# W2 staged in seven buffers, batch 1's third row block after group 0's last add, and earlier sums in the last group

## The chip, the cores and the metric

The kernel runs on one core of a Trainium2 chip. The metric is the device time of one execution in microseconds (us). The kernel before has a median of 313.59 us over six runs (312.78 to 314.56).

The engines are named as in the profile: PE is TensorE's matmuls and PEld its weight loads, DVE is VectorE, ACT is ScalarE, POOL is GpSimd, SP is SyncE, which here only issues transfers. DMA engines move data between HBM and the on-chip memory SBUF; matmuls write to PSUM.

## The reference

Two stages, eight batches of 576 positions, eight heads of 64, model width 512, hidden width 2048:

```python
def _attn_ref(q, k, v):                       # [8, 8, 576, 64] each
    scores = (1.0 / np.sqrt(D)) * np.matmul(q, k.transpose(0, 1, 3, 2))
    rel = pos[:, None] - pos[None, :]
    mask = (rel >= 0) & (rel < 64)            # a causal window of 64 positions
    scores = np.where(mask, scores, -1e9)
    attn = softmax(scores)
    return np.matmul(attn, v)

def _moe_ref(x, g_ln, w_ch1, w_ch2):          # x: [8, 576, 512], heads side by side
    xn = (x - mean) / np.sqrt(var + 1e-06) * g_ln
    ch = np.maximum(xn @ w_ch1, 0.0) @ w_ch2  # 512 -> 2048 -> 512
    return x + ch
```

Inputs and output are float32; the kernel computes its matmuls in float16 with float32 sums in PSUM.

## The kernel before, in words

**Tiling.** The first 512 positions of each batch make a group of four row blocks of 128 (`kb` or `j` 0 to 3): groups 0 to 7. The last 64 positions of all eight batches together make group 8, the last one. For a row block, `s_mm` makes the scores with 16 small matmuls (PE, L283) and their exponentials (ACT, L290), `s_mask` multiplies the mask in (DVE, L297), and `b_step` does 16 matmuls with V (PE, L317, into the one PSUM tile `xps`) and then, on DVE, the reciprocal of the sums (L320), the division into `xn` (L323), mean and variance (L325, L328) and, in groups 0 and 1, `z` (L338). From group 2 on `z_step` makes `z` on POOL (L342 to L345). `zt_step` brings `z` into `zT`, by PE and ACT (L357, L360) or by a transposing DMA (L353).

**The MLP of a group.** `mlp_units` gives a list of units, each some matmuls. Group 0: eight half blocks (`l1_half`, L528, eight matmuls each), eight whole blocks of the first layer (`l1`, L392), nine units `l2_two` (L543) that do the second layer of row blocks 0 and 1 together, piece by piece of W2, and eight units `l2` (L404) for row blocks 2 and 3, four parts each. After a row block's last part `add_out` adds the result to `xn` (DVE, L414), which frees the PSUM buffer, and `store` sends the rows out on SP's queue (L430). Group 1 has sixteen half blocks and sixteen `l2` parts. Groups 2 to 8 do the second layer in seven products instead of eight (`stage`, L469) with sums of the hidden activations `sS` (`s_sums`, DVE, L443) and sums of W2, `wT`, which `w2_sums` writes late in group 1 and in group 2. PSUM has two buffers `mm`, which hold the blocks `hps`, `hph`, `ch`, `pA` and `pB` in turn.

**Order.** There is no scheduler: each engine runs its instructions in the order in which the program was written out. At the end of the kernel a loop walks the units of group g; `at(i, f, ...)` puts work of the next batches (attention, loads, casts) behind unit i. Work put behind one unit runs in the order of the `at` calls.

**Loads and weights.** All loads go out on SP's queue, one after another, and a load waits there until its buffer is free. POOL casts everything to float16. W2 comes in eight pieces of 512 KB: `w2_load(i)` into one of the four buffers of the pool `pwst` (tag `wld`), `w2_cast(i)` into `w2s` (POOL, L201). Four loads were written first (L795), and load i + 4 after cast i (L800 to L803). Unit i of `l2_two` uses piece i for row block 0 and piece i - 1 for row block 1. The same four buffers hold `sS` from group 2 on. The tiles `wT[2]`, `wT[3]`, `wT[4]` are each as large as a piece, 4 KB in each partition.

**The last group.** Group 8 has its own order (`plan` in `mlp_units`): its first layer also runs in seven products (`l1_product`, L578), whose parts are kept by ACT (L590), added by DVE (L593) and rectified by DVE, POOL (L595) or ACT (L617). The second layer's stages follow, with `s_sums` between them: `s_sums(c0, c1, n)` makes sum n for chunks c0 to c1.

Of the kernel before, what the change touches and what calls it, by code (L numbers as in the profile page):

```python
# [10 lines left out]
FP32 = mybir.dt.float32  # L11
# [9 lines left out]
def kernel(  # L21
# [12 lines left out]
    DM = H * D  # L34
# [7 lines left out]
    XQ = 3  # L42
# [4 lines left out]
    p_wst = ctx.enter_context(tc.tile_pool(name="pwst", bufs=4))  # L47
# [23 lines left out]
    wT = {i: p_const.tile([128, NHC // 2, DM // 2], FP16, tag=f"wT{i}", name=f"wT{i}") for i in (2, 3, 4)}  # L71
# [119 lines left out]
                                    op0=ALU.mult, op1=ALU.mult)  # L191

    def w2_load(i):
        t = p_wst.tile([128, 2, DM], FP32, tag="wld", name=f"w2s_{i}")
        wst[("w2", i)] = t
        nc.sync.dma_start(
            out=t, in_=moe_w_ch2[256 * i:256 * (i + 1), :].rearrange("(c p) d -> p c d", p=128),
        )
# [184 lines left out]
    def mlp_units(g, split=0, two=False, seven=True):  # L383
# [48 lines left out]
        def s_sums(c0, c1, *which):  # L432
            if not sS:
                for n in range(1, 5):
                    sS[n] = p_wst.tile([128, NHC // 2, 256], FP16, tag="wld", name=f"sS{n}_{g}")
            c = slice(c0, c1)
            a11, a12 = hv[:, c, 0, 0:256], hv[:, c, 1, 0:256]
            a21, a22 = hv[:, c, 0, 256:512], hv[:, c, 1, 256:512]
            s1, s2, s3, s4 = (sS[n][:, c, :] for n in range(1, 5))
            for n in which:  # L440
                o, x, y, op = {1: (s1, a21, a22, ALU.add), 2: (s2, s1, a11, ALU.subtract),
                               3: (s3, a11, a21, ALU.subtract), 4: (s4, a12, s2, ALU.subtract)}[n]
                nc.vector.tensor_tensor(out=o, in0=x, in1=y, op=op)  # L443
# [40 lines left out]
        def stage(n, p):  # L484
            product(n, p)
            if last and n == 3:
                post_c(0, p)
                if p:
                    store_rest(0, slice(256, DM), None)
                return  # L490
            if p == 0:
                return
            if n == 1:
                post("A", 0, 0)
            elif n == 2:
                post("B", 0, 0)
                if last:
                    store_rest(0, slice(0, 256), nc.sync)
            elif n == 6:
                post("A", 0, 1)  # L500
            elif n == 7:
                post("A", 2, 1)
                if last:
                    post_c(2, 0)
                    post_c(2, 1)
                else:
                    post("C", 2, 1)
                post("A", 2, 0)
            elif n == 4:
                post("B", 2, 0)  # L510
                if last:
                    store_rest(2, slice(0, DM), None)
                else:
                    store(2)
                    store(3)
            elif n == 3:
                post("C", 0, 1)
                tbank["shared"] = False
                tbank["n"] = 0
                store(0)  # L520
                store(1)
# [89 lines left out]
        def l1_c(d):  # L611
            l1_product(7, d)
            l1_sum(l1_quad(d, 1, 1), "A", "s5", d)
# [5 lines left out]
        if last:  # L619
            def plan():  # L620
                yield
                l1_b(0)
                for d in range(1, 4):
                    l1_a(d)
                    l1_c(d - 1)
                    l1_b(d)
                    l1_e(d - 1)
                s_sums(0, 4)
                stage(1, 0)
                l1_c(3)  # L630
                s_sums(0, 4, 1)
                s_sums(4, 8, 1)
                stage(1, 1)
                l1_e(3)
                s_sums(0, 4, 2)
                stage(2, 0)
                s_sums(4, 8, 2)
                stage(2, 1)
                stage(6, 0)
                s_sums(0, 4, 3)  # L640
                stage(6, 1)
                s_sums(4, 8, 3)
                stage(5, 0)
                s_sums(0, 4, 4)
                stage(5, 1)
                s_sums(4, 8, 4)
                for n in (7, 4, 3):
                    for p in range(2):
                        stage(n, p)
                yield  # L650
            l1_a(0)
            return plan(), s_sums
# [139 lines left out]

    load_qk(1, 0)
    load_v(1, 0, 2)
    for i in range(4):  # L795
        w2_load(i)
    cast_qk(1, 0)
    cast_v(1, 0, 1)
    cast_v(1, 1, 2)
    for i in range(8):  # L800
        w2_cast(i)
        if i < 4:
            w2_load(i + 4)  # L803
    load_qk(1, 1)
    load_v(1, 2, 4)
    cast_qk(1, 1)
# [13 lines left out]
    for g in range(NGRP):  # L820
# [4 lines left out]
        units, s_sums = mlp_units(g, (8, 16)[g] if g < 2 else 0, g == 0, g > 1)  # L825
        slots = [[] for _ in range(len(units) + 1)]

        def at(i, f, *a):
            slots[min(i, len(slots) - 1)].append((f, a))

        b = g + 1
        if g == 0:
            at(0, b_step, 0, 3)
            at(1, zt_step, 0, 2)
            at(3, zt_step, 0, 3)
            at(4, newton, 0, 0, 4)
            at(11, t_main, 1, 0, 0, 1)
            at(12, t_main, 1, 1, 0, 1)
            at(13, vB_cur, 1, 0, 1)
            at(13, vB_prev, 1, 0, 1)  # L840
            at(13, vB_cur, 1, 1, 1)
            at(13, vB_prev, 1, 1, 1)
            at(16, s_mm, 1, 0)
            at(16, s_mask, 1, 0)
            at(17, s_mm, 1, 1)
            at(17, s_mask, 1, 1)
            at(18, b_step, 1, 0)
            at(21, b_step, 1, 1)
            at(22, zt_step, 1, 0)
            at(24, zt_step, 1, 1)  # L850
            at(26, t_main, 1, 0, 1, 0)
            at(27, t_main, 1, 1, 1, 1)
            at(28, vB_cur, 1, 2, 0)
            at(28, vB_prev, 1, 2, 1)
            at(29, vB_cur, 1, 3, 0)
            at(29, s_mm, 1, 2)
            at(29, s_mask, 1, 2)
            at(30, s_mm, 1, 3)
            at(30, s_mask, 1, 3)
            at(30, load_v, 2, 0, 4)  # L860
            at(31, b_step, 1, 2)
        if g == 1:
            at(0, cast_qk, 2, 0)
            at(0, cast_qk, 2, 1)
            at(1, b_step, 1, 3)
            at(2, zt_step, 1, 2)
            at(13, newton, 1, 0, 4)
            at(5, zt_step, 1, 3)
            at(4, alloc_v, 2)
            at(4, alloc_qkT, 2)  # L870
            at(4, alloc_vB, 2)
            at(5, cast_v, 2, 0, 4)
            at(5, make_vB, 2)
            at(4, t_main, 2, 0, 0)
            at(4, t_main, 2, 1, 0)
            at(6, t_main, 2, 0, 1)
            at(6, t_main, 2, 1, 1)
            at(25, w2_sums, 3, 0, 4)
            at(28, w2_sums, 3, 4, 8)
            for j in range(4):  # L880
                at((9, 13, 16, 19)[j], s_mm, 2, j)
                at((10, 14, 17, 20)[j], s_mask, 2, j)
                at((13, 17, 20, 23)[j], b_step, 2, j)
                at((13, 17, 20, 23)[j], z_step, 2, j)
                at((18, 21, 24, 27)[j], zt_step, 2, j)
            at(3, load_qk, 3, 0)
            at(4, load_qk, 3, 1)
            at(7, load_v, 3, 0, 4)
            at(8, alloc_qkT, 3)
            at(8, cast_qk, 3, 0)  # L890
            at(10, cast_qk, 3, 1)
            at(14, alloc_v, 3)
            at(14, cast_v, 3, 0, 2)
            at(14, cast_v, 3, 2, 4)
            at(17, alloc_vB, 3)
            at(17, make_vB, 3)
            at(31, s_mm, 3, 0)
            at(31, s_mask, 3, 0)
            for i, (x, half) in zip((12, 24, 12, 28), ((0, 0), (1, 0), (0, 1), (1, 1))):
                at(i, t_main, 3, x, half, 0)  # L900
            at(40, load_qk, 4, 0)
            at(40, load_qk, 4, 1)
            at(40, load_v, 4, 0, 4)
# [28 lines left out]
        if g > 1 and n < B:  # L932
            at(16, cast_qk, n, 1, (1,) if n >= XQ else (0, 1))
            at(20, alloc_v, n)
            at(20, cast_v, n, 0, 2)
            at(21, cast_v, n, 2, 4)
            at(21, alloc_vB, n)
            at(21, make_vB, n)
            for i, (x, half) in zip((13, 17, 13, 21) if n >= XQ else (17, 19, 21, 25),
                                    ((0, 0), (1, 0), (0, 1), (1, 1))):  # L940
                at(i, t_main, n, x, half, 0)
            at(27, s_mm, n, 0)
            at(28, s_mask, n, 0)
            if n + 1 < B:
                at(40, load_qk, n + 1, 0)
                at(40, load_qk, n + 1, 1)
                at(40, load_v, n + 1, 0, 4)
# [60 lines left out]
```

The softmax here doesn't subtract the row's maximum and nothing guards it: scores larger than these inputs give would overflow.

## Time and profile before

The profiled execution took 314.48 us, of which 312.7 us lie between its first and its last instruction (the span).

| engine | busy us | share of the span |
|---|---|---|
| PE | 298.3 | 95% |
| DVE | 217.9 | 70% |
| POOL | 170.8 | 55% |
| ACT | 153.1 | 49% |

Costly groups of instructions on PE: L392 96.3 us (416 matmuls, 380 ns each as recorded, overlapping), L404 23.1 us, L528 23.4 us. W2's loads take 5.1 us each from issue to landing, in the median of the eight. The granted clock of PE was 0.998 of full speed on the mean.

A timeline row gives start, duration, engine, line, operation, out<-in, shapes and count; a row of several instructions covers them from the first start to the last end. Brackets hold the idle time of the engine just before it and what ended it. Matmuls overlap, so each is recorded longer than the step to the next one.

### The profile page before, as it was taken

What the parts mean: (1) busy time and instruction counts of PE and PEld (TensorE: products, weight loads), DVE (VectorE), ACT (ScalarE), POOL (GpSimd) and SP (SyncE); (2) the same over time, 40 slices, a digit from 0 to 9 for tenths busy, and PEclk for the clock granted to TensorE, in tenths of its full rate; (3) what the DMA queues carried; (4) which work ended last, traced back from release to release, by engine and by line L of the source; (5) the groups of instructions that cost most, each with busy time, mean ns of one, the idle gap of its engine ahead of it and who ended that gap; (6) DMA issues with size and microseconds to landing.
All of it is one profiled execution on the core that took longest, in us unless ns stands there. A gap on an engine that the chain in (4) does not pass through costs nothing.

```text
span 312.7 us, 7625 instructions
## 1 busy us (share of the span) xinstructions
PE 298.3 (95%) x3089; PEld 198.4 (63%) x3089; DVE 217.9 (70%) x411; ACT 153.1 (49%) x258; POOL 170.8 (55%) x255
## 2 busy tenths in 40 slices
PE   7988989899999999999999989999999999999992
PEld 4556535598454468646954776459646855788882
DVE  0687675856665996589666945896569685877882
ACT  2486624487326742866157526772375048315500
POOL 7578666454951798279805964598236506204300
PEclk9999999999999999999999999999999999999999
DMA  8999999999776996897189997993690393003013
GB/s 192 270 386 288 336 310 283 290 293 217 148 170 201 248 185 127 264 293 123 34 258 286 194 151 203 322 144 64 203 183 17 53 205 132 2 0 136 0 37 101
DMA packets 109893, 57.43 MB, mean 184 GB/s; under 512 B 79841, under 2 KB 100833, under 8 KB 109858
## 3 DMA queue, kind: packets, MB, share of 16 engines
q1 hardware_dynamic: 108800, 53.75, 69.5%
q0 software_dynamic: 768, 2.80, 3.7%
q8 instruction: 24, 0.39, 0.5%
q10 hardware_dynamic: 290, 0.40, 0.4%
q14 instruction: 11, 0.09, 0.1%
HBM read 38.80 MB, written 9.44 MB: 154 GB/s over the span
## 4 chain that ended last, share of the span: by engine, by line
PE 69%; DMA 12%; DVE 7%; POOL 4%; SPq 4%; issue 2%; ACT 1%; POOLq 0%; ACTq 0%
PE hps L392 23%; PE pA L469 9%; PE pC L469 7%; PE pB L469 6%; PE ch L404 6%; DMA qk<-in_k_dram 4%; DMA w2s<-in_moe_w_ch_dram 4%; PE hph L528 4%; PE xps L317 3%; PE sc L283 3%; DVE sS L443 2%; PE lA L578 2%; SPq L141 2%; PE tp L226 2%; DMA zT<-z 2%
## 5 line engine op out<-in xcount | busy, mean ns | idle before, releaser
L392 PE MATMUL hps<-zT,w1g 128*128 128x512 f16 x416 | 96.3, 380 | 0.0
L396 ACT ACTIVATE hrT<-hps 128x512 f16<-128x512 f32 x104 | 62.3, 599 | 38.6 <-PE hps L392 35.1
L392 PEld LDWEIGHTS <-w1g 128*128 128x128 f16 x416 | 38.3, 98 | 41.9 <-issue 0.9
L290 ACT ACTIVATE pt<-sc 128x512 f16<-128x512 f32 x72 | 39.0, 595 | 28.9 <-DVE xn L476 15.6
L469 PEld LDWEIGHTS <-sS 128*128 128x128 f16 x448 | 43.1, 98 | 5.7 <-DVE sS L443 0.7
L342 POOL TENSOR_SCALAR rsz<-mvg 128x1 f32<-128x1 f32 x28 | 10.7, 382 | 60.0 <-DVE mvg L328 59.4
L128 POOL CAST qk<-qk 128x1024 f16<-128x1024 f32 x32 | 34.9, 1102 | 13.4 <-DMA qk<-in_k_dram 7.2
L469 PEld LDWEIGHTS <-hrT 128*128 128x128 f16 x336 | 32.5, 98 | 5.3 <-ACT hrT L617 0.3
L212 ACT COPY qkT<-tp 128x1024 f16<-128x1024 f16 x16 | 16.1, 1012 | 34.6 <-PE tp L226 25.5
L297 DVE TENSOR_TENSOR pt<-pt,mask 128x1024 f16<-128x1024 f16 x32 | 26.0, 818 | 9.2 <-ACT pt L290 9.1
L476 DVE TENSOR_TENSOR xn<-pA,xn 128x512 f32<-128x512 f32 x28 | 19.2, 686 | 18.4 <-PE pA L469 18.4
L345 POOL TENSOR_SCALAR z<-xn,rsz 128x512 f16<-128x512 f32 x28 | 25.0, 892 | 4.6 <-DMA zT<-z 1.8
L469 PE MATMUL pA<-wT,sS 128*128 128x256 f16 x224 | 27.1, 273 | 0.2 <-DVE sS L443 0.2
L469 PE MATMUL pC<-w2s,sS 128*128 128x256 f16 x224 | 26.8, 273 | 0.0
L320 DVE RECIPROCAL rcp<-xps 128x8 f32<-128x8 f32 x36 | 7.4, 205 | 26.7 <-PE xps L317 26.7
L325 DVE BATCH_NORM_STATS2 stats<-xn 128x6 f32<-128x512 f32 x36 | 25.0, 695 | 1.2
L323 DVE TENSOR_TENSOR xn<-xps,rcp 128x512 f32<-128x512 f32 x36 | 24.9, 691 | 1.2
L528 PE MATMUL hph<-zT,w1g 128*128 128x256 f16 x192 | 23.4, 273 | 2.1 <-ACT zT L360 1.1
L443 DVE TENSOR_TENSOR sS<-hrT 128x512 f16<-128x512 f16 (+1 forms) x40 | 24.5, 614 | 0.6 <-ACT hrT L396 0.6
L404 PE MATMUL ch<-w2s,hrT 128*128 128x512 f16 x96 | 23.1, 380 | 0.0
L528 PEld LDWEIGHTS <-w1g 128*128 128x128 f16 x192 | 18.2, 98 | 5.1 <-issue 2.2
L317 PEld LDWEIGHTS <-pt 128*64 128x64 f16 x576 | 12.2, 110 | 13.7 <-issue 5.7
(108 smaller groups left out, 450.5 us busy)
## 6 DMA issues: line engine op xcount, KB each, us to landing
out_dram<-xn SPq DMA_DIRECT2D x33, 256.0 KB, 2.8
qk<-in_q_dram SPq DMA_DIRECT2D x16, 512.0 KB, 6.4
qk<-in_k_dram SPq DMA_DIRECT2D x16, 512.0 KB, 7.4
v<-in_v_dram SPq DMA_DIRECT2D x32, 256.0 KB, 6.5
w2s<-in_moe_w_ch_dram SPq DMA_DIRECT2D x12, 512.0 KB, 5.7
w1s<-in_moe_w_ch_dram SPq DMA_DIRECT2D x4, 512.0 KB, 6.7
tk<-in_k_dram SPq DMA_DIRECT2D x8, 256.0 KB, 4.6
tv<-in_v_dram SPq DMA_DIRECT2D x8, 256.0 KB, 5.7
```

The source lines that it names most:

```text
L128: nc.gpsimd.tensor_copy(out=dst[:, :].rearrange("p (a j) e d -> p a e j d", j=j), in_=t[:, :].rearrange("p (a e j d) -> p a e j d", e=2, j ...
L290: nc.scalar.activation(out=o, in_=i, func=AF.Exp, bias=0.0, scale=scale)
L297: nc.vector.tensor_tensor(out=ptv, in0=ptv, in1=mb, op=ALU.mult)
L323: nc.vector.tensor_tensor(out=xn, in0=xps[:, :, 0:D], in1=rcp_b, op=ALU.mult)
L325: nc.vector.bn_stats(out=stats, in_=xv)
L345: nc.gpsimd.tensor_scalar(out=z, in0=xv, scalar1=rs, scalar2=nm, op0=ALU.mult, op1=ALU.add)
L392: nc.tensor.matmul(out=hps, lhsT=w1g[:, kc, 128 * hc:128 * (hc + 1)], rhs=zT[g][:, kc, :], start=(kc == 0), stop=(kc == NKC - 1),)
L396: nc.scalar.activation(out=hrT[:, hc, :], in_=hps, func=AF.Relu, bias=0.0, scale=1.0)
L404: nc.tensor.matmul(out=ch[kb], lhsT=hrT[:, hc, 128 * kb:128 * (kb + 1)], rhs=w2s[:, hc, :], start=(hc == 0), stop=(hc == NHC - 1),)
L443: nc.vector.tensor_tensor(out=o, in0=x, in1=y, op=op)
L469: nc.tensor.matmul(out=o, lhsT=a[:, c, 128 * p:128 * p + 128], rhs=wv[:, c, :], start=(first and (p == 0 or split_c) and c == 0), stop=(c ...
L528: nc.tensor.matmul(out=hps[:, e], lhsT=w1g[:, kc, 128 * hc:128 * (hc + 1)], rhs=zT[g][:, kc, 256 * half:256 * half + 256], start=(kc == 0) ...
```

## The change

Five edits:

1. W2's pieces 4, 5 and 6 are staged in `wT[2]`, `wT[3]` and `wT[4]`, which nothing uses until `w2_sums` writes them in group 1. Seven loads are written first, and load 7 after cast 0, where before loads 4 to 7 came after casts 0 to 3.
2. `b_step(1, 2)` moves from behind unit 31 of group 0 to behind its last unit, so that its matmuls stand behind the last four of the second layer, and its DVE work behind the last `add_out` of group 0.
3. `b_step(2, 0)` and `z_step(2, 0)` move from behind unit 13 to behind unit 14 of group 1. On PE they come behind the scores of row block 1 and one half block. The order on DVE and POOL stays.
4. In group 2 the two transposes of batch 4's keys move from behind units 17 and 21 to behind units 18 and 22 (one stage of eight matmuls later each).
5. In the last group sum 1 of chunks 0 to 4 is made behind the first layer's third step (d = 2), and the second sums come one or two steps sooner. The sums of chunks 0 to 4 and of 4 to 8 thus no longer stand next to each other on DVE.

No transfer, cast or matmul is added or left out.

```diff
     def w2_load(i):
-        t = p_wst.tile([128, 2, DM], FP32, tag="wld", name=f"w2s_{i}")
+        if 4 <= i < 7:
+            t = wT[i - 2][:, :, :].rearrange("p c n -> p (c n)").bitcast(FP32).rearrange("p (c n) -> p c n", c=2)
+        else:
+            t = p_wst.tile([128, 2, DM], FP32, tag="wld", name=f"w2s_{i}")[:, :, :]
...
                     l1_e(d - 1)
-                s_sums(0, 4)
+                    if d == 2:
+                        s_sums(0, 4, 1)
                 stage(1, 0)
+                s_sums(0, 4, 2)
                 l1_c(3)
-                s_sums(0, 4, 1)
                 s_sums(4, 8, 1)
                 stage(1, 1)
                 l1_e(3)
-                s_sums(0, 4, 2)
+                s_sums(4, 8, 2)
                 stage(2, 0)
-                s_sums(4, 8, 2)
                 stage(2, 1)
...
-    for i in range(4):
+    for i in range(7):
         w2_load(i)
...
     for i in range(8):
         w2_cast(i)
-        if i < 4:
-            w2_load(i + 4)
+        if i == 0:
+            w2_load(7)
...
-            at(31, b_step, 1, 2)
+            at(33, b_step, 1, 2)
...
-                at((13, 17, 20, 23)[j], b_step, 2, j)
-                at((13, 17, 20, 23)[j], z_step, 2, j)
+                at((14, 17, 20, 23)[j], b_step, 2, j)
+                at((14, 17, 20, 23)[j], z_step, 2, j)
...
-            for i, (x, half) in zip((13, 17, 13, 21) if n >= XQ else (17, 19, 21, 25),
+            for i, (x, half) in zip((13, 18, 13, 22) if g == 2 else (13, 17, 13, 21),
                                     ((0, 0), (1, 0), (0, 1), (1, 1))):
                 at(i, t_main, n, x, half, 0)
```

## The prediction

> **What bounds the kernel now.** I read the chain of waits first, then the table of stretches, then each engine's timeline where TensorE stands still.
>
> ```profile
> PE 69%; DMA 12%; DVE 7%; POOL 4%; SPq 4%; issue 2%; ACT 1%; POOLq 0%; ACTq 0%
> 30.00:62.00 32.00, 29.48 (x283) 15.35 (x281) 21.49 (x32) 14.23 (x24) 19.68 (x23) 1.00 0.99 301
> 62.00:96.00 34.00, 34.00 (x380) 22.75 (x379) 20.05 (x45) 17.84 (x31) 19.27 (x30) 1.00 0.82 197
> 282.00:308.00 26.00, 24.80 (x220) 20.98 (x218) 20.56 (x39) 8.04 (x14) 5.95 (x4) 1.00 0.17 54
> ```
>
> The first line is the chain by engine, the others are stretches (their length, then busy us of PE, PEld, DVE, ACT, POOL, the granted clock, the DMA share, GB/s). TensorE sets the pace and hardly rests: from 62 to 96 us not at all. It rests 2.5 us between 30 and 62, and 1.2 us in the last group. The edits aim at those two stretches, so their stalls are the most that can be won directly. The DMA engines are full (0.99) in the first of them.
>
> In TensorE's timeline the rests are in the square brackets, with who ended them:
>
> ```profile
> 41.63 3.02 PE L543 MATMUL ch<-w2s,hrT 128*128 128x512 f16 x12
> 45.92 1.02 PE L543 MATMUL ch<-w2s,hrT 128*128 128x512 f16 x4 [0.89 <-POOL w2s L201]
> 47.56 1.46 PE L543 MATMUL ch<-w2s,hrT 128*128 128x512 f16 x6 [0.39 <-POOL w2s L201]
> 60.34 1.03 PE L528 MATMUL hph<-zT,w1g 128*128 128x256 f16 x8 [0.74 <-ACT hrT L533]
> 297.94 2.09 PE L469 MATMUL pA<-wT,sS 128*128 128x256 f16 x16 [0.18 <-DVE sS L443]
> ```
>
> Two rests wait for a W2 cast, one for a PSUM buffer, one for a sum of the last group. The casts behind the first two, in GpSimd's timeline:
>
> ```profile
> 40.72 1.18 POOL L201 CAST w2s<-w2s 128x1024 f16<-128x1024 f32 x1 [0.26 <-DMA w2s<-in_moe_w_ch_dram]
> 42.54 1.04 POOL L201 CAST w2s<-w2s 128x1024 f16<-128x1024 f32 x1 [0.64 <-DMA w2s<-in_moe_w_ch_dram]
> 44.83 1.04 POOL L201 CAST w2s<-w2s 128x1024 f16<-128x1024 f32 x1 [1.25 <-DMA w2s<-in_moe_w_ch_dram]
> 46.47 1.04 POOL L201 CAST w2s<-w2s 128x1024 f16<-128x1024 f32 x1 [0.60 <-DMA w2s<-in_moe_w_ch_dram]
> ```
>
> These are pieces 4 to 7; each waits for its load.
>
> **W2 in seven buffers.** The count of loads, casts and bytes stays. Loads 4, 5, 6 were issued at 35.83, 37.08 and 39.22, each after the cast that freed its buffer, and load 7 at 40.48; now 4 to 6 follow load 3 (about 32.5) and 7 follows cast 0 (ends 35.81). The loads behind them on SP's queue (q and k of batch 1, 40.90 before) go out near 36.3. The transfers are in a line, so going out sooner helps only where the line ran dry. Casts 3 to 4 are 1.30 apart (39.42, 40.72): the line was full, no gain. Cast 5 came 1.82 after 4, cast 6 2.29 after 5, cast 7 1.64 after 6. I leave 5 where it is and set 6 and 7 at 1.30: start 43.84 and 45.14, cast 7 done at 46.18. TensorE, unhindered, wants piece 6 at 44.95 and piece 7 at 46.05, so it starts piece 7 at 46.2 instead of 47.56: 1.36 us sooner.
>
> That lead meets a new wait at once. The next block (L404, 49.08) takes the PSUM buffer that the first L414 must empty, and L414 stands on VectorE behind z of rows 1 of batch 1:
>
> ```profile
> 46.99 0.80 DVE L338 TENSOR_SCALAR z<-xn,mvg 128x512 f16<-128x512 f32 x1
> 48.19 1.61 DVE L414 SCALAR_TENSOR_TENSOR xn<-ch,rstdg,xn 128x512 f32<-128x512 f32 x2 [0.40 <-PE ch L543]
> ```
>
> VectorE's chain to that z starts at the attention matmuls of 44.58, which don't move while piece 5 stays. So L414 can start at 47.8 at best when z takes 0.80, end 0.75 later at 48.55, and L404 starts at 48.6: **0.5 us** sooner. With z in 0.49 (the row at 60.70) it is 0.8; with pieces 5 to 7 all in time it could be 1.4; with z pushed behind the cast of q it is 0. I take 0.5, nearest to the row, and keep 0 to 1.4.
>
> z's 0.80 lies beside the cast of 46.47, and the mask at 57.61 (1.26 instead of 0.69) beside a cast of 57.29 to 58.33; both end 0.3 to 0.5 after that cast. The Trainium skill has a rule for it that speaks against this part: "SBUF — State Buffer", section "SBUF: two separate sides", says that GpSimd and some VectorE instructions take a port pair as an exclusive lock, and the loser waits for the whole instruction. By that rule the cast of q (then about 46.7 to 47.7) would hold z to 48.0 or later and this part would be worth 0.0 to 0.3, against 0.5 by the row.
>
> **Rows 2 of batch 1 behind the final add.** VectorE's rows now:
>
> ```profile
> 57.61 1.26 DVE L297 TENSOR_TENSOR pt<-pt,mask 128x1024 f16<-128x1024 f16 x1 [0.92 <-ACT pt L290]
> 59.03 0.69 DVE L323 TENSOR_TENSOR xn<-xps,rcp 128x512 f32<-128x512 f32 x1
> 60.70 0.49 DVE L338 TENSOR_SCALAR z<-xn,mvg 128x512 f16<-128x512 f32 x1
> 61.10 0.75 DVE L414 SCALAR_TENSOR_TENSOR xn<-ch,rstdg,xn 128x512 f32<-128x512 f32 x1
> 61.80 0.21 DVE L320 RECIPROCAL rcp<-xps 128x8 f32<-128x8 f32 x1
> ```
>
> The final add (L414, 61.10) waits behind five attention instructions though its matmuls ended at 58.74; until 61.85 group 1 has one PSUM buffer, so its second block waits for ScalarE (60.34) and its third for the add (61.90). In the new order, in the old clock: the last four L404 run before the attention matmuls and end near 58.35; the add runs 58.80 to 59.55; the second block starts at 59.6 (was 60.34); rcp and xn end at 60.44, which lets the attention of rows 3 start at 60.5 (was 61.31); the third block starts at 60.9 (was 61.90). Then z of rows 2 ends at 61.9 (was 61.19) and its transposes, ready on TensorE at 61.75, start at 61.95 (were 62.77). That is **0.8 us**. Bounds: 0.3 if the mask is held longer, 1.15 (the three starts above, with no wait for z).
>
> **Batch 2's rows 0 one unit later.** Its 16 attention matmuls (75.27) go behind 16 score matmuls (0.34) and one block of eight (0.87): 1.2 us later. TensorE has other work, so nothing direct: 0. The cover is on GpSimd: z of rows 0 starts about 1.0 later, and GpSimd is nearly solid from 77.92 to 91.74 with its four z steps and two casts, with 0.78 idle before the last z; so the last z slips about 0.2. Its transpose landed at 94.72 and group 2 begins at 95.24. With that cover gone it would cost up to 1.0. In return, the V shifted by DMA (landed 74.98, 0.3 before its first use) can't stop a TensorE that is 1.3 us ahead.
>
> **Key transposes of group 2 one stage later.** TensorE waits 0.30 at 114.17 for the key cast. Later by eight matmuls (0.87) that wait goes, but the next stage waits for L476, which ends at 116.45 after VectorE has worked without a break since 110.56, and the transposes at 120.70 for a z on that same chain. So 0, between -0.1 (the copy of the second half now ends near 120.8) and 0.3.
>
> **Last group's sums.** VectorE and TensorE now:
>
> ```profile
> 290.48 0.29 DVE L595 TENSOR_SCALAR hrT<-hrT 128x512 f16<-128x512 f16 x1
> 291.14 0.69 DVE L593 TENSOR_TENSOR hrT<-lB,s1sums 128x512 f16<-128x512 f32 x1 [0.36 <-ACT s1sums L590]
> 295.40 1.28 DVE L443 TENSOR_TENSOR sS<-hrT 128x1024 f16<-128x1024 f16 x2
> 297.20 1.28 DVE L443 TENSOR_TENSOR sS<-sS,hrT 128x1024 f16<-128x1024 f16 x2
> ```
>
> A sum costs VectorE 0.60 (two in 1.28, overlapped). The first goes into the 0.36 idle at 290.77, so it pushes the L593 of 291.14 to 291.39, and with it the reuse of a PSUM buffer by TensorE at 292.52: a loss of 0.25 carried to 297. The second goes into the 0.56 idle before 294.47 and costs nothing more. With two sums gone from the row at 297.20, the last second sum ends near 297.55, before TensorE wants it (297.85). The 16 matmuls at 297.94 then lose their waits, 0.35 before and 0.16 inside (2.09 instead of 1.91). Net **0.25**, between -0.1 and 0.5.
>
> **Sum.** 0.5 + 0.8 + 0 + 0 + 0.25 = 1.55 us. TensorE is unbroken from 62 to 110, and loads of later groups go out behind stores that follow TensorE, so I let the lead last to the end. The profiled execution took 314.48 (span 312.7, 1.8 around it) and becomes 312.9. The median of six is 313.59, 0.89 under that execution; the same saving gives **312.0**.
>
> **The rivals.**
> 1. W2 gives nothing: z and L414 on VectorE take the wait's place completely. For it: z at 46.99 and the mask at 57.61, both longer beside a cast; against it: L414's 0.40 idle. 313.59 - 1.05 = 312.5. Chance 0.12.
> 2. All stalls go: W2 1.4, final add 1.15, sums 0.5, key wait 0.3. For it: TensorE has no other rest before 114. Against: VectorE's chain above. 310.2. Chance 0.14.
> 3. The lead is won and given back before 125 us: at group 2's start (transpose landed only 0.5 ahead, GpSimd's z late) or in VectorE's unbroken run to 118. Only the sums' 0.25 is left: 313.3. Chance 0.15.
> 4. Slower: collisions of GpSimd's casts with VectorE's sums. In group 2 the sum at 111.96 takes 1.26 beside casts where a free one of 114.31 takes 0.41, so each new collision on the bound chain costs 0.85. A shift of TensorE against the casts repeats in groups 2 to 6; from two collisions in all (1.7) it outweighs the 1.55, and with three the time is 314.6. Against it: casts and sums both follow TensorE. Chance 0.06.
>
> **How the numbers follow.** My forecast has 0.53, with its own range 311.2 to 312.6. A measurement of this kernel can't tell less than 0.3% (0.94 us) from no change. Faster by more than that (under 312.65): forecast, rival 2 and 0.07 of rival 1, 0.74. Same: rival 3 and the rest of 1, 0.20. Slower: 0.06. The range reaches down into rival 2 (310.5) and up past rival 3 (313.4), leaving some 0.08 and 0.10 outside.
>
> **What would show it.** Casts 6 and 7 starting near 43.8 and 45.1, no rest before L543 in TensorE's row; the first L414 directly behind z, L404 near 48.6; the last L414 of group 0 before rcp, the second block of group 1 resting under 0.4; transposes of rows 2 at about 1.3 sooner than 62.77; 16 matmuls of pA in 1.91 near the end. I am wrong if casts 6 and 7 still come at 44.8 and 46.5, if TensorE rests at the first attention of batch 2 or at group 2's start, or if VectorE's sums there grow.

## The result, and the profile after

The changed kernel has a median of 311.35 us over 21 runs (310.75 to 313.05), beside 313.42 us for the kernel before in the same session. The ratio is 0.9934, with an interval of 0.9919 to 0.995: faster by 0.7%, or 2.1 us (1.6 to 2.5). The profiled execution took 311.79 us, with a span of 310.0 (before 314.48 and 312.7).

Lines of the program are three higher than before: L546 is the old L543, L417 the old L414, and so on. The first line is again the chain of waits by engine; then the stretches, with the last one taken 2.6 us sooner so that it holds the same work.

```profile
PE 77%; DMA 11%; DVE 5%; SPq 3%; POOL 1%; issue 1%; ACT 0%; POOLq 0%; ACTq 0%
30.00:62.00 32.00, 30.28 (x295) 16.23 (x293) 21.24 (x33) 14.30 (x25) 19.82 (x23) 1.00 0.97 300
62.00:96.00 34.00, 34.00 (x375) 22.12 (x372) 21.49 (x45) 18.58 (x31) 19.36 (x30) 1.00 0.81 201
279.40:305.40 26.00, 24.88 (x223) 21.44 (x221) 20.89 (x39) 8.08 (x15) 5.95 (x4) 1.00 0.18 55
```

TensorE's rest between 30 and 62 fell from 2.5 to 1.7 us. The DMA share and the rate over that stretch are nearly what they were (0.99 and 301 before). In TensorE's timeline two of the four rests are still there and two are gone:

```profile
45.86 1.02 PE L546 MATMUL ch<-w2s,hrT 128*128 128x512 f16 x4 [0.81 <-POOL w2s L204]
47.62 1.46 PE L546 MATMUL ch<-w2s,hrT 128*128 128x512 f16 x6 [0.51 <-POOL w2s L204]
58.61 1.92 PE L531 MATMUL hph<-zT,w1g 128*128 128x256 f16 x16
115.57 1.91 PE L472 MATMUL pA<-wT,sS 128*128 128x256 f16 x16 [0.34 <-DVE xn L479]
295.41 1.91 PE L472 MATMUL pA<-wT,sS 128*128 128x256 f16 x16
```

The rests for W2 stand at the same places (0.89 and 0.39 before). From start to start of the matmuls a rest is some 0.16 longer than its bracket; further down the longer figure is meant where no line is shown. The one of 0.74 at 60.34 is gone: the first and second block of group 1 now run as one row of 16. The 16 matmuls of pA near the end take 1.91 without a rest. A rest of 0.34 at 115.57 is new; before, one of 0.30 stood at 114.17, in front of the key transposes.

The casts that TensorE waits for, on GpSimd:

```profile
40.83 1.05 POOL L204 CAST w2s<-wT 128x1024 f16<-128x1024 f32 x1 [0.39 <-DMA wT<-in_moe_w_ch_dram]
42.56 1.04 POOL L204 CAST w2s<-wT 128x1024 f16<-128x1024 f32 x1 [0.68 <-DMA wT<-in_moe_w_ch_dram]
44.77 1.04 POOL L204 CAST w2s<-wT 128x1024 f16<-128x1024 f32 x1 [1.17 <-DMA wT<-in_moe_w_ch_dram]
46.52 1.04 POOL L204 CAST w2s<-w2s 128x1024 f16<-128x1024 f32 x1 [0.71 <-DMA w2s<-in_moe_w_ch_dram]
```

They start within 0.11 us of where they started before. The new buffers are in use (w2s<-wT), and yet each cast waits for its load as long as it did, to within 0.13 us. SP's queue, first of the kernel before, then of the changed one:

```profile
29.56 11.29 SPq L196 DMA_DIRECT2D w2s<-in_moe_w_ch_dram  x8
40.90 0.46 SPq L89 DMA_DIRECT2D qk<-in_q_dram  x1
41.42 1.42 SPq L89 DMA_DIRECT2D qk<-in_k_dram  x1
```

```profile
32.56 2.26 SPq L199 DMA_DIRECT2D wT<-in_moe_w_ch_dram  x3
36.28 0.47 SPq L89 DMA_DIRECT2D qk<-in_q_dram  x1
36.79 4.60 SPq L89 DMA_DIRECT2D qk<-in_k_dram  x1
```

Pieces 4 to 7 were issued at 32.56, 33.14, 34.06 and 35.87 instead of 35.83, 37.08, 39.22 and 40.48. They landed at 40.71, 42.08, 44.65 and 46.40, against 40.59, 42.06, 44.71 and 46.35. The 3 to 5 us that SP won it spent in the issues further on: that of k took 4.60 instead of 1.42, and that of the first load of V behind it 4.65 instead of 3.25. The load of q of rows 1, issued 4.62 sooner, landed at 47.98 instead of 48.12.

The landings alone don't tell what the earlier issue did. This is the stretch from 42 to 44 us, first of the kernel before, then of the changed one (the last two numbers are the DMA share and GB/s):

```profile
42.00:44.00 2.00, 1.91 (x10) 0.78 (x8) 1.93 (x4) 0.00 (x0) 1.04 (x1) 1.00 0.87 250
42.00:44.00 2.00, 1.85 (x9) 0.78 (x8) 1.93 (x4) 0.00 (x0) 1.04 (x1) 1.00 1.04 360
```

So the line did run partly dry before, which the share of 0.99 over 32 us hides, and with the early issue it stays full. By the rate it is so in every execution of this case with whole pieces: 344 to 369 GB/s here in the seven with edit 1, 250 to 291 in the five without. W2's packets (2 KB each, 2048 in all; nothing else in this stretch has that size) also move sooner: by 43.0 us, 3904 of the 4096 KB are done in the changed kernel and 3646 in the kernel before. But a piece has landed only when its last packet is in. In the changed kernel W2's last 14 packets came one at a time from 44.28 to 45.66, while other packets already carried the next loads; in the kernel before the last one ended at 45.86. The bytes came sooner, the last packets hardly. What held those back isn't shown.

VectorE around the last add of group 0 (L417, the old L414):

```profile
57.67 0.94 DVE L300 TENSOR_TENSOR pt<-pt,mask 128x1024 f16<-128x1024 f16 x1 [0.92 <-ACT pt L293]
58.53 0.74 DVE L417 SCALAR_TENSOR_TENSOR xn<-ch,rstdg,xn 128x512 f32<-128x512 f32 x1
59.42 0.69 DVE L326 TENSOR_TENSOR xn<-xps,rcp 128x512 f32<-128x512 f32 x1
61.09 0.49 DVE L341 TENSOR_SCALAR z<-xn,mvg 128x512 f16<-128x512 f32 x1
```

The add starts 2.57 us sooner (58.53 for 61.10), z of rows 2 only 0.39 later (61.09 for 60.70). The transposes of rows 2 start at 61.73 instead of 62.77.

### Where the time came from

The order of TensorE's matmuls is nearly the same in all the kernels of this case, so the span can be cut at the starts of the same matmuls and the lengths compared. This makes a ledger, worked out from the traces (us). **Start**: up to the 16th matmul of L546 (42.7 before). **W2**: from there to the first L407 (49.1 before). **Add**: to the second block of group 1 (60.3). **V**: to the last matmul of group 1's first layer (77.6). **Z**: to group 2's first matmul (95.2). **Key**: from a matmul at 110.9 to one at 128.0. **T**: from 176.0 to 192.1. **Sums**: from 280.0 to 303.0. What lies between is 15.69, 47.96 and 87.90 us in all of them, within 0.02.

| run | edits | Start | W2 | Add | V | Z | Key | T | Sums | span |
|---|---|---|---|---|---|---|---|---|---|---|
| before | none | 42.72 | 6.35 | 11.27 | 17.29 | 17.60 | 17.08 | 16.09 | 23.07 | 312.7 |
| after | all | 42.69 | 6.44 | 10.36 | 17.21 | 17.60 | 17.13 | 14.69 | 22.65 | 310.0 |
| e1_w2_only | 1 | 43.10 | 5.77 | 11.45 | 17.28 | 17.60 | 17.07 | 14.69 | 23.06 | 311.3 |
| e2_add_only | 2 | 43.46 | 6.03 | 10.36 | 17.29 | 17.60 | 17.07 | 14.69 | 23.06 | 310.9 |
| e3_sums_only | 5 | 42.61 | 5.72 | 11.27 | 17.58 | 17.60 | 17.08 | 14.69 | 22.64 | 310.4 |
| e4_no_w2 | 2 to 5 | 42.69 | 6.48 | 10.36 | 17.71 | 17.62 | 17.12 | 14.70 | 22.65 | 310.5 |
| e5_all_again | all | 42.52 | 5.39 | 10.36 | 17.21 | 17.60 | 17.13 | 14.70 | 22.65 | 308.8 |
| e6_no_w2_again | 2 to 5 | 42.69 | 5.59 | 10.36 | 17.21 | 17.60 | 17.13 | 14.69 | 22.65 | 309.2 |
| e7_no_3 | 1, 2, 4, 5 | 42.46 | 6.35 | 10.62 | 17.49 | 17.60 | 17.13 | 14.78 | 22.65 | 310.3 |
| e8_no_4 | 1, 2, 3, 5 | 42.78 | 5.29 | 10.36 | 17.83 | 17.60 | 17.07 | 14.69 | 22.65 | 309.5 |
| e9_half_w2 | all, less W2 | 43.53 | 5.46 | 10.36 | 17.21 | 17.60 | 17.14 | 14.70 | 22.65 | 309.8 |
| e10_half_w2_late | 2 to 5, less W2 | 42.93 | 5.21 | 10.36 | 17.21 | 17.60 | 17.13 | 14.70 | 22.65 | 309.0 |
| e11_split_cast | all, casts split | 42.44 | 5.24 | 10.69 | 17.30 | 17.64 | 17.13 | 16.56 | 22.65 | 311.9 |
| e12_split_u15 | all, rows 0 later | 43.01 | 6.71 | 10.49 | 16.81 | 19.64 | 17.13 | 14.70 | 22.65 | 312.3 |

Between the two profiled executions 2.69 us went: 0.91 in Add, 1.40 in T, 0.42 in Sums, 0.08 in V, with 0.09 lost in W2 and 0.05 in Key (the start and the end make up the rest).

**The 1.40 in T is not shown to be the change's.** In the profile before, TensorE stood there for a z on GpSimd, which waited for a transposing transfer. The lines are GpSimd's and TensorE's timeline and the chain of waits:

```profile
178.81 5.17 DMA zT<-z
184.15 0.76 POOL L345 TENSOR_SCALAR z<-xn,rsz 128x512 f16<-128x512 f32 x1 [1.76 <-DMA zT<-z]
184.97 0.40 PE L357 MATMUL ztp<-ident,z 128*128 128x128 f16 x4 [1.24 <-POOL z L345]
```

In the changed kernel:

```profile
181.60 1.02 POOL L348 TENSOR_SCALAR z<-xn,rsz 128x512 f16<-128x512 f32 x1
182.68 0.40 PE L360 MATMUL ztp<-ident,z 128*128 128x128 f16 x4
```

That transfer took 5.17 us in the first and 4.19 in the second. The wait is missing in e1 to e10 and in e12, with any of the edits or without them, and it is back in e11, which has all of them and where the transfer took 5.67. So it comes and goes with the execution, in 2 of 14; how often each kernel has it, one profile of each can't say. Without it the two profiled executions differ by 1.28 us. That is less than the 2.07 between the medians, and the interval of that difference (1.6 to 2.5) doesn't hold it.

### The profile page after: what moved, and what is told of

It reads as the page before. It is cut to its first block, busy times and chain, and to the rows that moved or that the text cites. A ratio compares the mean times of both kernels' runs of the same rounds, so it can differ in the third digit from the quotient of the medians.

```text
span 310.0 us, 7624 instructions
## 1 busy us (share of the span) xinstructions
PE 297.4 (96%) x3089; PEld 198.6 (64%) x3089; DVE 219.2 (71%) x411; ACT 153.0 (49%) x258; POOL 171.3 (55%) x255
## 4 chain that ended last, share of the span: by engine, by line
PE 77%; DMA 11%; DVE 5%; SPq 3%; POOL 1%; issue 1%; ACT 0%; POOLq 0%; ACTq 0%
PE hps L395 25%; PE pA L472 11%; PE pB L472 7%; PE pC L472 7%; PE ch L407 7%; DMA w2s<-in_moe_w_ch_dram 5%; PE hph L531 5%; DMA qk<-in_q_dram 4%; PE xps L320 3%; PE sc L286 3%; PE lA L581 2%; PE tp L229 2%; SPq L141 2%; DMA w1s<-in_moe_w_ch_dram 2%; DVE sS L446 2%; SPq L89 1%
## 5 line engine op out<-in xcount | busy, mean ns | idle before, releaser
L395 PEld LDWEIGHTS <-w1g 128*128 128x128 f16 x416 | 38.4, 98 | 41.9 <-issue 0.9
L479 DVE TENSOR_TENSOR xn<-pA,xn 128x512 f32<-128x512 f32 x28 | 19.2, 686 | 17.2 <-PE pA L472 17.2
L407 PE MATMUL ch<-w2s,hrT 128*128 128x512 f16 x96 | 22.9, 380 | 0.0
L147 POOL CAST vA<-v 128x1024 f16<-128x1024 f32 (+2 forms) x19 | 17.3, 928 | 6.3 <-DMA v<-in_v_dram 6.3
```

The lines of the kernel that those rows point to most:

```text
L395: nc.tensor.matmul(out=hps, lhsT=w1g[:, kc, 128 * hc:128 * (hc + 1)], rhs=zT[g][:, kc, :], start=(kc == 0), stop=(kc == NKC - 1),)
L407: nc.tensor.matmul(out=ch[kb], lhsT=hrT[:, hc, 128 * kb:128 * (kb + 1)], rhs=w2s[:, hc, :], start=(hc == 0), stop=(hc == NHC - 1),)
```

## The experiments

**One edit at a time.** Against the kernel before: e1 has only edit 1, e2 only edit 2, e3 only edit 5. e4 has all but edit 1:

```diff
-    for i in range(7):
+    for i in range(4):
         w2_load(i)
...
-        if i == 0:
-            w2_load(7)
+        if i < 4:
+            w2_load(i + 4)
```

with each piece in `p_wst` again.

> The kernel before with the W2 edit alone. Theory A (the DMA engines, not the issue, set when W2's pieces land): casts 6 and 7 start at 44.8 and 46.4 as before, TensorE rests as before at both pieces, and the time is the before kernel's within 0.3 us. Theory B (the prediction: the line ran dry, and the gain is only hidden in the changed kernel): casts at about 43.8 and 45.1, the time 0.5 us lower. Theory C (W2 in the line hurts what stands behind it): the time is 0.5 us or more higher.

> The kernel before with b_step(1, 2) behind the last unit of group 0 alone. Theory A: the rests at group 1's second and third blocks fall from 1.2 us to under 0.2 in all, the lead is 0.9 to 1.0 us by the third block and 0.6 to 0.9 after batch 2's rows 0 (which come sooner and may wait for the V shifted by DMA), the time 0.6 to 1.1 us lower. Rival: the lead is given back before group 2, the time is the before kernel's within 0.3 us.

> The kernel before with the earlier sums of the last group alone. Theory A: TensorE's last 40 us shorten by 0.3 to 0.4 us, the wait at pA (0.35 and 0.16 us) goes and 0.17 us comes at lA before. Rival: the inserted sum holds up lA by as much as is won, 0.0. By time alone it can hardly be told from no change.

> The changed kernel with the W2 edit undone. Theory A (W2 gives nothing): the time of the changed kernel within 0.3 us, that is 1.8 to 2.3 us under the kernel before. Theory B (W2 gives 0.5): 0.5 us above the changed kernel, 1.5 under the kernel before.

Measured, beside a median of 313.45 us before: e1 313.64 (ratio 0.9999, 0.9982 to 1.0016), e2 313.37 (1.001, 0.9986 to 1.0034), e3 313.29 (0.9997, 0.9976 to 1.0017), e4 312.84 (0.9982, 0.9957 to 1.0007). No edit alone is told from no change by its time. In the ledger two of them are plain: Add is 10.36 with edit 2 and 11.27 to 11.45 without; Sums is 22.65 with edit 5 and 23.06 without, to 0.01. The profiled executions of e1 to e3 lie 0.6 to 1.1 us under their medians, so other executions lose time that these don't show. For e2 that is a contradiction that stays open: 0.91 is 0.3%, and its interval leaves out anything below 0.9986. Against what was expected: e1's casts of pieces 6 and 7 started at 44.54 and 45.95 and its time is that of the kernel before, which is nearest to theory A; e2's rests went as in theory A, but its time didn't follow; e3's Sums fit theory A; e4 fits neither theory, being 0.6 us under the kernel before instead of 1.8 to 2.3 or 1.5.

e3 also shows what a lead runs into at 75 us. V of batch 2 is shifted by a transfer from GpSimd's queue, and the first attention matmul of batch 2 needs it. e3's lines of GpSimd and TensorE:

```profile
67.25 0.74 POOL L165 DMA_DIRECT2D vB<-vA  x1 [0.31 <-POOL vA L147]
74.81 0.19 PE L317 MATMUL xps<-vB,pt 128*64 128x65 f16 x1 [0.40 <-DVE rstdg L381]
```

The shift landed at 74.67, after 7.42 us. The name in the bracket misleads: the transfer ended just ahead of the matmul, and the profile put the wait down to a VectorE instruction. The whole wait was 0.56.

**The changed kernel again, and without edits 1, 3 and 4.** e5 is the changed kernel, e6 is e4 again, and e7 and e8 take back one move each:

```diff
-                at((14, 17, 20, 23)[j], b_step, 2, j)
-                at((14, 17, 20, 23)[j], z_step, 2, j)
+                at((13, 17, 20, 23)[j], b_step, 2, j)
+                at((13, 17, 20, 23)[j], z_step, 2, j)
...
-            for i, (x, half) in zip((13, 18, 13, 22) if g == 2 else (13, 17, 13, 21),
+            for i, (x, half) in zip((13, 17, 13, 21) if n >= XQ else (17, 19, 21, 25),
```

The first four lines of change are e7's, the last two e8's.

> The changed kernel once more, on the chip of the three runs beside it. Expected 2.0 us under the kernel before, with its fastest executions 1.6 us under the fastest of the kernel before.

> The changed kernel without the W2 edit, once more, because its first run was wide (311.9 to 317.9 us). Theory A (W2's edit gives nothing in itself, the first run's median was scatter): the median and the fastest executions within 0.3 us of the changed kernel's. Theory B (the W2 edit moves the loads behind W2 and so the V of batch 2, which bounds the lead): 0.6 to 1.0 us above the changed kernel, and the shifted V of batch 2 lands 1 us later (near 76.0 against 74.7).

> The changed kernel with b_step(2, 0) back behind unit 13. Theory A (the V of batch 2, shifted by DMA, lands at 74.6 to 76.0 in every kernel and stops a TensorE that comes sooner): TensorE waits 0.5 to 0.8 us at the first attention matmul of batch 2, and the lead of 0.95 us falls to 0.5, the time 0.4 to 0.6 above the changed kernel. Rival (the move was only a shift): no wait over 0.2, same time within 0.3.

> The changed kernel with the key transposes of group 2 back behind units 17 and 21. Theory A (VectorE's chain bounds the next stage, the edit gives nothing): TensorE waits 0.47 us at the transposes and 0.14 at pA after them instead of 0.50 at pA alone, and is at the same time at the stages behind; the time of the changed kernel within 0.3 us. Rival: 0.4 us above it.

Measured beside 313.15 us before: e5 311.62 (0.9952, 0.9933 to 0.9972), e6 311.85 (0.9957, 0.9938 to 0.9976), e7 312.18 (0.9970, 0.9954 to 0.9985), e8 312.04 (0.9962, 0.9945 to 0.9979). All four are faster than before, and their intervals overlap. Edits 2 to 5 without the first (e6) give 0.4%, as much as all of them do in e5 within what can be told apart. e4 and e6 are the same kernel, and their ratios are 0.9982 and 0.9957: that is how far two sessions of one kernel can lie apart.

Against what was expected: e5 came 1.5 us under the kernel before, not 2.0. e6 lies 0.2 over e5, and its shift of V landed at 74.54, not near 76.0: theory A. e7 lies 0.6 over e5, about as its theory A said, but not by the wait that it names: V's shift had landed at 74.09 and the matmul that needs it started at 74.55, without a rest before it. What e7 lost is in W2, Add and V, the last by a z that took 2.20 beside a cast of 1.89 at 63.5. e8 lies 0.4 over e5, which is its rival's number, but in the ledger edit 4 isn't where that comes from.

**Edit 3** doesn't hold the lead by itself. V is 17.21 in five of the eight kernels that have the edit, but 17.71 in e4 and 17.83 in e8; without it, 17.28 to 17.58. The means are 17.36 and 17.39. Where TensorE stood still at the first attention matmul of batch 2, it was when the shift landed that decided. e8, with the edit:

```profile
65.19 1.89 POOL L147 CAST vA<-v 128x2048 f16<-128x2048 f32 x1 [3.85 <-DMA v<-in_v_dram]
67.39 0.74 POOL L165 DMA_DIRECT2D vB<-vA  x1 [0.31 <-POOL vA L147]
75.10 0.19 PE L320 MATMUL xps<-vB,pt 128*64 128x65 f16 x1 [0.26 <-DMA vB<-vA]
```

GpSimd's cast waits 3.85 us for the load of V, the shift starts behind the cast and lands at 74.97. TensorE was 1.91 us ahead of the kernel before at 58.43 (the start of the second block of group 1), and the move puts the matmul 1.13 later (75.55 in the changed kernel, which was 0.85 ahead), so it was due at 75.27 + 1.13 - 1.91 = 74.49 and lost 0.61. In e4 TensorE was only 0.80 ahead, but the shift landed at 75.96. Over the executions it landed between 73.4 and 76.0. The two means hide that the leads with the edit were larger. Without the move the matmul would have been due 2.07 and 1.70 before 75.27 in e5 and e6, at 73.20 and 73.57, and V landed at 73.59 and 74.54: an estimate from these numbers, with the landing as it was, is that the edit saved 0.4 and 1.0 us there.

**Edit 4** costs 0.05 us: Key is 17.12 to 17.14 in the nine executions with it and 17.07 or 17.08 in the five without. The wait of 0.47 for the key cast before goes, and waits of 0.50 for L479 and 0.39 at the transposes of z take the place of 0.14 and 0.25.

**z and L417 on VectorE.** e7 and e8 are a pair that shows the limit behind W2. In both, pieces 6 and 7 came early (piece 7 landed at 44.85 and 45.33). Lines of e7, from GpSimd, VectorE and TensorE:

```profile
46.78 1.04 POOL L128 CAST qk<-qk 128x1024 f16<-128x1024 f32 x1 [0.77 <-PE ch L546]
46.82 1.28 DVE L341 TENSOR_SCALAR z<-xn,mvg 128x512 f16<-128x512 f32 x1
48.16 0.40 PE L360 MATMUL ztp<-ident,z 128*128 128x128 f16 x4 [0.64 <-DVE z L341]
48.81 1.45 PE L407 MATMUL ch<-w2s,hrT 128*128 128x512 f16 x6 [0.26 <-DVE xn L417]
```

Of e8:

```profile
47.30 1.04 POOL L128 CAST qk<-qk 128x1024 f16<-128x1024 f32 x1 [0.80 <-DMA qk<-in_q_dram]
46.87 0.49 DVE L341 TENSOR_SCALAR z<-xn,mvg 128x512 f16<-128x512 f32 x1
48.07 1.89 PE L407 MATMUL ch<-w2s,hrT 128*128 128x512 f16 x8
```

In e7 the cast of q starts 0.04 ahead of z, z takes 1.28 and ends 0.28 after the cast, and TensorE gives back all that W2 brought: W2 is 6.35, as before. In e8 z is over when the cast starts, takes 0.49, and W2 is 5.29. The Trainium skill ("SBUF — State Buffer", "SBUF: two separate sides") has GpSimd and some VectorE instructions take a port pair as an exclusive lock. A full lock would have ended e7's z at 48.31; it ended at 48.10, so the row agrees but for 0.2 us. The other order is seen in e1: z starts at 47.68 and takes 0.49, the cast of q starts at 47.75 and takes 1.31. Which mode z runs in, on which the page makes the lock depend, no run here shows.

**Half the bytes.** e9 loads only the first half of pieces 4 to 7; e10 does the same without edit 1, so that the loads go out late:

```diff
+        n = 1 if i >= 4 else 2
         nc.sync.dma_start(
-            out=t, in_=moe_w_ch2[256 * i:256 * (i + 1), :].rearrange("(c p) d -> p c d", p=128),
+            out=t[:, 0:n], in_=moe_w_ch2[256 * i:256 * i + 128 * n, :].rearrange("(c p) d -> p c d", p=128),
         )
...
+            for c in range(2):
+                nc.gpsimd.tensor_copy(out=w2s[:, 2 * i + c, :], in_=t[:, 0, :])
```

> All five edits, but of W2's pieces 4 to 7 only the first half is loaded, and both halves of the cast read it: the second half of those rows of W2 is left out. 1 MB less goes over the line. In the profiles so far the pieces landed at 40.7, 42.1, 44.7 and 46.4 whether they were issued at 32.6 to 35.9 or at 35.8 to 40.5, and q of rows 1 at 48.0. Theory (the line of transfers is full, and the bytes in front set the landing): at the 301 GB/s of that stretch each half piece (0.26 MB) is worth 0.87 us, so the pieces land near 39.8, 40.3, 42.0 and 42.9 and q near 44.5; TensorE's rests before L543 (0.3, 1.0, 0.7) go, a rest before the next block of L404 comes in (VectorE's z and L414), and the time is 0.3 to 0.8 us under that of the changed kernel. Rival 1 (one late packet on one of the 16 engines, of fixed length, holds piece 6): piece 6 still 2.3 us or more behind piece 5, landing 43.5 or later. Rival 2 (the landings come from the issues on SP, which stood in the q and v loads for 4.6 us each): landings as before within 0.5.

> As the run with half pieces, but without the first edit: pieces 4 to 7 are issued behind the casts that free their buffers (35.8, 37.1, 39.2, 40.5 in the profile before); the second half of those rows of W2 is left out. If only the bytes in front count, the pieces land as in the run with early issues, within 0.5 us, and the times are the same within 0.5 us. If a shorter line lets the early issue count (the line now runs dry), pieces 6 and 7 land 0.5 to 1.5 us later than there, and the time lies 0.2 to 0.6 us over it.

In e9 the half pieces landed at 41.04, 41.73, 42.41 and 43.12, in e10 at 39.61, 40.28, 42.17 and 43.20: pieces 6 and 7, issued 5.2 and 4.2 us later, came within 0.25 us of each other. That looks as if the issue didn't count, but the two lines weren't in the same state. From 38 to 42 us, first e9, then e10:

```profile
38.00:42.00 4.00, 3.87 (x60) 1.72 (x59) 1.52 (x4) 2.86 (x6) 2.54 (x3) 1.00 1.06 382
38.00:42.00 4.00, 3.83 (x60) 1.72 (x58) 3.69 (x5) 2.77 (x5) 3.86 (x5) 1.00 0.71 226
```

e9's line was full, and its pieces follow each other by 0.7; but it was late, with piece 2 landing at 39.09 (37.66 in e10). e10's line ran dry, and each piece landed 2.9 to 3.5 us behind its own issue. Counted from piece 2's landing, pieces 6 and 7 came 3.3 and 4.0 us later in e9, and 4.5 and 5.5 in e10. So with half the bytes the late issue did count, by 1.2 and 1.5 us, as the second reading in e10's expectation has it; that pieces 6 and 7 land together comes from e9's late line. For pieces 4 and 5, which are 1.4 later in e9, they don't agree within the 0.5 expected.

Both runs show that fewer bytes in front bring a piece sooner. Against the whole pieces of the changed kernel's first profile pieces 6 and 7 came 2.2 to 2.5 and 3.2 to 3.3 sooner, and q of rows 1 3.1 and 3.0 sooner. Against faster executions of the changed kernel (43.12 and 45.06 in e5) the gain is 0.7 to 1.9. Rival 1 of these runs (a late packet of fixed length) isn't seen in e9; in e10 piece 6 came 1.89 behind piece 5, but it was issued 1.62 behind it.

The times are 311.33 (ratio 0.992, 0.9893 to 0.9947) and 311.03 (0.9918, 0.9893 to 0.9943). Both intervals hold the changed kernel's 0.9934, so e9's gain of 0.3 to 0.8 us can't be told from none by the times. e10's lines from GpSimd and TensorE show what is left with W2 in time:

```profile
40.06 5.81 POOL L207 CAST w2s<-w2s 128x512 f16<-128x512 f32 x8
46.02 1.46 PE L549 MATMUL ch<-w2s,hrT 128*128 128x512 f16 x6
48.14 1.89 PE L410 MATMUL ch<-w2s,hrT 128*128 128x512 f16 x8 [0.26 <-DVE xn L420]
```

No rest stands before L549 any more, and the one before the next block (0.43 with its step) waits for VectorE's add. W2 is then 5.21, 1.14 under the profile before and 0.8 under the mean of the five executions without edit 1 (6.03).

**Two tries at a better kernel.** e11 casts the second half of pieces 6 and 7 on ScalarE; e12 puts rows 0 of batch 2 one more unit later (and splits no cast, whatever its label says):

```diff
+            at(20, w2_cast_act, 6)
             at(21, b_step, 1, 1)
+            at(21, w2_cast_act, 7)
...
-                at((14, 17, 20, 23)[j], b_step, 2, j)
-                at((14, 17, 20, 23)[j], z_step, 2, j)
+                at((15, 17, 20, 23)[j], b_step, 2, j)
+                at((15, 17, 20, 23)[j], z_step, 2, j)
```

> All five edits, and of W2's pieces 6 and 7 the second half is cast on ScalarE beside GpSimd's first half. A cast of a whole piece took 1.04 on GpSimd, so each is done about 0.5 sooner with its landing unchanged (44.7, 46.4). Theory (TensorE waits for landing plus cast, the landing is fixed): rests before L543 of 0.97 and 0.67 shrink by 0.4 in all or more, time 0.2 to 0.5 us under the changed kernel, ratio to before 0.992. Rival (z and L414 on VectorE, or V of batch 2, take the wait's place): rests shrink, time within 0.2 of the changed kernel (ratio 0.9935 to 0.995). Other side: ScalarE stands at its cast until the piece lands and holds the copies behind it (hrT and the score exponentials), TensorE rests more there, time 0.3 or more above the changed kernel.

> All five edits, and rows 0 of batch 2 (attention matmuls and z) one more unit later, at 15 instead of 14: the attention goes behind another block of eight L531. With edit 3 absent the attention's first matmul stood 0.2 to 0.6 us for V of batch 2 in the executions whose lead was large. Theory (at unit 14 the wait is gone save in a quick execution): no wait for V here either, last z and transpose of batch 2 about 0.2 to 0.9 later; time as the changed kernel within 0.3, ratio 0.993 to 0.996. Rival (V still clamps at unit 14 in most executions): 0.3 to 0.6 under the changed kernel. Other side (GpSimd's z chain, which I named as the cover, is short): group 2 starts up to 1.0 later, ratio 0.996 to 0.999.

e11: 312.80 us (0.9967, 0.9946 to 0.9988), 1.5 us over the changed kernel's median and not the gain expected. Its profile shows the local effect: no rest for pieces 6 and 7, W2 5.24, with the pieces landing at 42.89 and 44.83. But it lost 0.33 in Add, 1.87 in T and 1.0 behind the last matmul. Whether the split has a part in the wait in T wasn't tried.

e12: 312.99 us (0.9993, 0.997 to 1.0017). The step too far shows at group 2's start. GpSimd and TensorE:

```profile
79.19 1.04 POOL L147 CAST vA<-v 128x1024 f16<-128x1024 f32 x1 [0.51 <-DMA v<-in_v_dram]
81.58 1.04 POOL L147 CAST vA<-v 128x1024 f16<-128x1024 f32 x1 [1.35 <-DMA v<-in_v_dram]
84.33 0.76 POOL L348 TENSOR_SCALAR z<-xn,rsz 128x512 f16<-128x512 f32 x1
93.20 0.76 POOL L348 TENSOR_SCALAR z<-xn,rsz 128x512 f16<-128x512 f32 x1
96.66 2.58 PE L395 MATMUL hps<-zT,w1g 128*128 128x512 f16 x11 [1.49 <-DMA zT<-z]
```

The same z steps in the changed kernel:

```profile
79.67 0.76 POOL L348 TENSOR_SCALAR z<-xn,rsz 128x512 f16<-128x512 f32 x1
90.44 0.76 POOL L348 TENSOR_SCALAR z<-xn,rsz 128x512 f16<-128x512 f32 x1
```

At unit 15 the first z stands behind two casts of V of batch 3, which wait for their loads. It starts 4.66 later, the last one 2.76 later, and TensorE waits 1.65 (1.49 in the bracket) for the transpose of it. At unit 14 the transpose landed at 93.79, 0.51 before its use at 94.30: that was all the room there was. e12's Z is 2.04 longer than the changed kernel's, but 0.40 of this are the 16 attention matmuls, which moved into it from V. This is the other side of e12's expectation, with a higher price.

No kernel of these that does the whole computation is faster than the changed one.

## Why the prediction was right or wrong

The forecast was 312.0 us, the median is 311.35, on the side foreseen and within the range. The forecast's case was the one that came, but its sum was put together from one term too large and two too small.

- **W2, 0.5.** This step failed, by the sign that the prediction gave for it: casts 6 and 7 still came at 44.77 and 46.52. "Set 6 and 7 at 1.30" supposed that the gaps between casts 5, 6 and 7 were the line running dry because loads went out late. It did run dry (250 GB/s from 42 to 44 us, 360 with the edit), and W2's bytes did move sooner. But the gaps stayed (2.21 and 1.75 us), because a piece's last packets came as late as before. Over all executions with whole pieces, piece 6 landed at 43.72 on the mean of the seven with edit 1 and at 44.32 on that of the five without, piece 7 at 45.45 and 45.80; the two sets overlap. Where pieces came sooner, the next wait could take the gain. The W2 stretch is 5.29 to 6.71 in the six profiled executions with edit 1 and whole, unsplit pieces (mean 5.99), and 5.59 to 6.48 in the five without (mean 6.03). On the mean nothing is left of the term; with this scatter a few tenths either way aren't excluded.
- **The new wait behind W2** was seen rightly where pieces come early (e7, e9, e10, e11): L407 behind L417 behind z. Its size depends on z: with 0.49 the stretch can be 1.06 shorter than in the profile before (e8; I had 0.8), with 1.28 nothing is left. The skill's rule, which I had put at 0.0 to 0.3, was the better guide for e7, and the row for e8; both occur.
- **The final add, 0.8.** Right in place and mechanism; it measures 0.91 in the ledger. The second block's rest went (no rest where 0.4 was allowed), and the transposes of rows 2 came 1.04 sooner where I had 0.8.
- **Rows 0 of batch 2, 0.** Right as a sum. The cover named, GpSimd's chain of z and the transpose 0.5 ahead of group 2, held with 0.51 to spare; with it gone the price was 1.65 (e12), not "up to 1.0", because two casts that wait for loads stand in between. That V "can't stop" a TensorE 1.3 us ahead held only for a landing near 75.0: in e4 V came at 75.96 and stopped one that was 0.8 ahead, and in e8 the lead was 1.9. The move paid in some executions (0.4 and 1.0 in e5 and e6 by the estimate above), which the sum put at nothing.
- **Key transposes, 0.** Right: a loss of 0.05, by the two waits named.
- **Last sums, 0.25.** 0.42 in every execution. The loss of 0.25 that I took off became 0.10 (the step before one block of L581 went from 0.17 to 0.27), and of the rests of 0.35 and 0.16 nothing stayed.
- **The lead lasts to the end.** Right: behind 96 us every stretch has the same length with the lead and without it, to 0.1 us, but for T, for Sums by edit 5, and for the end of e11.
- **Against which time.** I made the sum against a profiled execution 0.89 over its median. That execution held the wait of 1.40 in T, which I hadn't looked for; as I took the saving from the median, it did no harm.

The terms shown add to 0.91 + 0.42 - 0.05 = 1.28 us. The medians say 1.6 to 2.5 in the first session, 0.9 to 2.1 for e5, and for edits 2 to 5 alone 0.7 to 1.9 (e6) and -0.2 to 1.3 (e4). So 1.28 agrees with the repeats and not with the first session, where at least 0.3 us, and 0.8 by the medians, isn't accounted for. That the median comes as near to the forecast as 0.65 us is in part luck: without W2's 0.5 the same sum gives 312.5.

Of the rivals, the first (W2 nothing, 312.5) was nearest to what happened, by another cause: the last packets of the pieces, and only in some executions z. The second (all stalls go) didn't come; the third (given back before 125 us) happened only in part, at V in e4 and e8; the fourth (slower) had no trace.

## What to carry to other kernels

Before loads are issued sooner, look at the DMA share in short stretches and at when the last packet of each load comes: here a share of 0.99 over 32 us held 0.87 in two of them, and though the early issue filled that, W2's last packets came hardly sooner. And look at what waits next, since a gain of a load can end at another engine. Before a step is moved behind another unit, list what then stands ahead of it on every queue that it uses, above all instructions that wait for a load. And where a saving is 0.1 to 0.3%, cut several traces at the same matmuls: times of whole executions couldn't tell single edits apart here, while the stretches that no edit touched repeated to 0.02 us and showed which part was the execution's own.

## What the runs showed of the hardware

- The issue of a load can itself take long on SP behind other loads: 4.60 us for k in the changed kernel, 3.25 for a load of V before, beside 0.47 for q just ahead of the first.
- The landing of equal pieces of 512 KB in one line isn't even: piece 6 came 1.32 to 3.36 us behind piece 5 in the twelve executions with whole pieces, and 2.57 and 2.65 in the two main ones. A 16 KB packet of the instruction queue took 1.12 and 0.92 us in these just then, but a like one (0.88 to 1.21) is in all fourteen, those with piece 6 1.3 behind too, so it alone doesn't tell the late ones from the others.
- A transposing transfer took 2.5 to 3.4 us in the median of an execution, and 3.5 to 5.7 for the first of those near 177 us; in the two executions where that one took over 5.1, TensorE stood still.
- VectorE's z takes 0.49 us alone, up to 1.34 beside a cast of 1.04 on GpSimd, and 2.20 beside one of 1.89.
